# Eight of sixteen on-chip copies of one batch issued from ACT's queue instead of SP's, in a fused attention and expert kernel

## The chip, the cores and the metric

One core of one Trainium2 chip runs the whole program. The metric is the device time of one execution in microseconds (us); less is better. Before the change the median of three runs is 466.92 us (466.87 to 467.25).

The core has five instruction streams that run at once, each in order: TensorE (PE), VectorE (DVE), ScalarE (ACT), GpSimd (POOL) and SyncE (SP). They wait for each other on semaphores. DMA transfers are issued by an instruction on one of these streams and then run by themselves; in the kernel before, SP issues all of them.

## The reference

```python
def sm_attn(qq, kk, vv):
    s = scale * np.matmul(qq, kk.transpose(0, 1, 3, 2))
    s = s - np.max(s, axis=-1, keepdims=True)
    a = np.exp(s)
    a = a / (np.sum(a, axis=-1, keepdims=True) + 1e-09)
    return np.matmul(a, vv)
p_packed = sm_attn(p, k, v)            # 32 packed queries for each head
out = sm_attn(q, p_packed, p_packed)   # 576 queries for each head
...
h = np.maximum(np.maximum(x @ w1, x @ w2), x @ w3)   # x: 4608 x 512, w: 512 x 768
return (h @ w_out).astype(np.float32)
```

There are 8 batches, 8 heads, 576 rows and a head width of 64, all in float32.

## The kernel before, in words

The batches b = 0 to 7 go through the same stages, and the stages of neighbouring batches are interleaved by hand. A stage is a Python generator; one word of a table runs it to its next `yield`, so the table is the order in which every engine gets its instructions. `START` (lines 48 to 73) holds batches 0 and 1 and the beginning of batch 2, and also the words `w` and `C` that load and convert the weights of the two expert layers. `LOOP` (lines 77 to 85) holds one round for each of b = 2 to 7. A word is a letter of a stage, the batch, and further indices.

The stages that matter here:

- `A` (`weigh`, line 261): the exponentials of the packed queries' scores, 128 x 576, in two tiles `a`. For batches 0 and 1 they are transposed on PE (`turn`, line 286).
- `X` (`spread`, line 305): from batch 2 on, DVE transposes 32 x 32 blocks into `x` (line 313), and sixteen SBUF-to-SBUF DMAs move these blocks to the partitions where PE wants them, in the tile `xt` (line 319). Eight of them move 5 blocks and eight 4 blocks for each of 32 partitions. A batch's third word `X` emits the sixteen DMAs.
- `V` (`values`, line 324): 80 small matmuls `av` with `xt` as their weights (line 337), a scaling on DVE to `pp`, then `K` (`packed`, line 349): a transpose on PE (line 352) and a copy to `pt`.
- `Q` (`queries`, line 356): the second scores, with `q` tiles that `load_q` (line 169) brought from memory (issue at line 174).
- `P` and `N` (`project`, `layer_in`): the first expert layer. Its sums `mi` (line 475) are most of PE's work; `E` (`maximum`, line 481) copies the first sum out of PSUM on ACT or DVE (`copy`, lines 129 and 131) and takes the maximum with the others on DVE (line 489).
- `C` (`convert`, line 177): two activations on ACT (lines 188 and 193), a shift on DVE (line 202) and an add on POOL (line 206) put the words of a weight block `wi` in order. `load_w` (issue at line 153) fetches the next `wi` into one of six slots.

The stretch of `START` in which batch 2's DMAs are emitted is this (lines 60 and 61); its `X2` is the third one:

```
... P05 N05 N05 N05 E040
w60 C60 B10g B10 B11 H00 N10 C61 E041 P11 Z20 E050 H00v X2 C60 C60 E041 C61 E050 P11 V201 Z21 V201 N11 N11 K2
```

`N05` are the sums of block 5, `E050` starts with the copy of the first of them on ACT, `V201` runs the `av` matmuls, and `w64`, `w65`, `q21`, `q20`, `w62`, `w63` in the next line are loads issued by SP.

The pool tag `b` has eight slots. The `q` tiles of batch 2 reuse slots that the `av` matmuls and the sixteen DMAs read, so these loads wait for both.

Of the kernel before, what the change touches and what calls it, by code (L numbers as in the profile page):

```python
# [20 lines left out]
B, H, S, D, NP = 8, 8, 576, 64, 32  # L21
# [67 lines left out]
def fused_kernel(ctx: ExitStack, tc: tile.TileContext, kp, qt, va, vb, wi, wo, out):  # L89
# [14 lines left out]
    nc = tc.nc  # L104
# [200 lines left out]
    def spread(b):  # L305

        x = pool.tile([P, NT, R, NP], F32, name=f"x{b}", tag="b", bufs=NB)
        for r in range(R):
            nc.vector.transpose(out=x[:, :, r], in_=a1[b, r][0].rearrange("p (t y) -> p t y", y=NP))
            yield 1
        at = pool.tile([P, SF + 1, 4, R, NP], F32, name=f"xt{b}", tag="b", bufs=NB)
        for c in range(4):
            n = len(range(c, NT, 4))
            for i in range(4):
                nc.sync.dma_start(out=at[NP * c:NP * c + NP, 0:n, i], in_=x[NP * i:NP * i + NP, c::4])  # L319
        for r in range(R):  # L320
            a1t[b, r] = at[:, :, :, r]
        yield 0
# [282 lines left out]
    def weigh_and_turn(b, r):  # L605
# [4 lines left out]

    stages = {
        "S": scores, "A": weigh_and_turn, "Z": invert, "X": spread, "V": lambda b, *rs: values(b, rs), "K": packed, "Q": queries,
        "B": attend, "C": convert, "P": project, "N": layer_in, "E": maximum, "H": halves,
        "O": layer_out, "F": finish, "W": weights,
# [77 lines left out]
```

## Time and profile before

| | |
|---|---|
| time, median of three runs | 466.92 us (466.87 to 467.25) |
| span of the profiled execution | 464.4 us |
| PE busy | 455.2 us (98%) |
| DVE busy | 333.5 us (72%) |
| POOL busy | 247.9 us (53%) |
| ACT busy | 159.9 us (34%) |
| DMA queues | 55.66 MB, all of the kernel's own transfers on one queue |

The time of the profiled execution itself is not listed beside its span. The span runs from the first to the last instruction, and the median of the three runs is 2.5 us longer than it. Busy times are sums over the span. DMA issues are not counted as busy, so ACT's and SP's streams can be occupied where the table shows nothing. An engine that waits shows up as the idle time before an instruction, with the engine or DMA that ended it; the chain of waits follows these back from the last instruction.

### The profile page before, as it was taken

What the parts mean: (1) busy time and instruction counts of PE and PEld (TensorE: products, weight loads), DVE (VectorE), ACT (ScalarE), POOL (GpSimd) and SP (SyncE); (2) the same over time, 40 slices, a digit from 0 to 9 for tenths busy, and PEclk for the clock granted to TensorE, in tenths of its full rate; (3) what the DMA queues carried; (4) which work ended last, traced back from release to release, by engine and by line L of the source; (5) the groups of instructions that cost most, each with busy time, mean ns of one, the idle gap of its engine ahead of it and who ended that gap; (6) DMA issues with size and microseconds to landing.
All of it is one profiled execution on the core that took longest, in us unless ns stands there. A gap on an engine that the chain in (4) does not pass through costs nothing.

```text
span 464.4 us, 11561 instructions
## 1 busy us (share of the span) xinstructions
PE 455.2 (98%) x4724; PEld 404.9 (87%) x4724; DVE 333.5 (72%) x698; ACT 159.9 (34%) x341; POOL 247.9 (53%) x213
## 2 busy tenths in 40 slices
PE   7999998999999999999999999999999999999996
PEld 3477887899899898998899988998989988998996
DVE  1799987888887678566887479766786668845552
ACT  2787856535322126022331025121260223302130
POOL 0468875574542675526572384706764275725832
PEclk9999999999999999999999999999999999999999
DMA  8999846010316430256004450065202540020002
GB/s 313 398 382 355 321 98 230 1 58 25 95 66 195 135 119 1 80 160 233 2 27 152 87 211 2 27 199 155 94 1 94 151 116 1 28 76 1 2 6 97
DMA packets 35780, 55.66 MB, mean 120 GB/s; under 512 B 17296, under 2 KB 26512, under 8 KB 35728
## 3 DMA queue, kind: packets, MB, share of 16 engines
q1 hardware_dynamic: 35728, 54.93, 35.4%
q8 instruction: 37, 0.61, 0.5%
q14 instruction: 15, 0.12, 0.1%
HBM read 41.94 MB, written 9.44 MB: 111 GB/s over the span
## 4 chain that ended last, share of the span: by engine, by line
PE 88%; DMA 5%; SPq 3%; DVE 3%; issue 1%; ACT 1%; DVEq 0%
PE mi L475 44%; PE mo L544 29%; PE pw L439 6%; PE idle L143 2%; SPq L319 2%; PE s L366 2%; PE av L337 2%; DMA wi<-in_wi 2%; PE s L253 2%; DMA q<-in_qt 1%; DMA kt<-in_kp 1%; PE tp L296 0%; DMA xt<-x 0%; SPq L159 0%; PE pa L337 0%
## 5 line engine op out<-in xcount | busy, mean ns | idle before, releaser
L475 PE MATMUL mi<-a2h,ph 128*128 128x288 f32 x576 | 173.5, 301 | 0.8 <-DVE pl L452 0.6
L475 PE MATMUL mi<-a2l,ph 128*128 128x288 f32 x576 | 169.9, 295 | 0.0
L475 PE MATMUL mi<-a2h,pl 128*128 128x288 f32 x576 | 169.6, 295 | 0.0
L489 DVE TENSOR_TENSOR r<-mi,r 128x288 f32<-128x288 f32 x192 | 84.4, 452 | 57.8 <-PE mi L475 55.3
L475 PEld LDWEIGHTS mi<-a2h,ph 128*128 128x128 f32 x576 | 108.0, 188 | 13.4 <-issue 7.0
L475 PEld LDWEIGHTS mi<-a2l,ph 128*128 128x128 f32 x576 | 108.0, 188 | 0.2
L475 PEld LDWEIGHTS mi<-a2h,pl 128*128 128x128 f32 x576 | 108.1, 188 | 0.0
L513 POOL TENSOR_TENSOR r<-r 128x288 f32<-128x288 f32 (+1 forms) x47 | 50.4, 1083 | 81.3 <-DVE r L489 65.5
L129 ACT COPY r<-mi 128x288 f32<-128x288 f32 x73 | 29.0, 399 | 185.8 <-PE mi L475 185.7
L450 ACT ACTIVATE ph<-pw 128x384 fp32r<-128x384 f32 (+1 forms) x67 | 40.2, 631 | 46.5 <-PE pw L439 43.5
L452 DVE SCALAR_TENSOR_TENSOR pl<-pw,ph 128x384 fp32r<-128x384 f32 (+1 forms) x67 | 46.2, 713 | 9.5 <-ACT ph L450 9.2
L544 PE MATMUL mo<-ych,xl 128*128 128x288 f32 x144 | 42.5, 295 | 0.0
L544 PE MATMUL mo<-ych,xh 128*128 128x288 f32 x144 | 42.4, 294 | 0.0
L544 PE MATMUL mo<-ycl,xh 128*128 128x288 f32 x144 | 42.3, 294 | 0.0
L439 PE MATMUL pw<-w_sb,pt 64*32 64x384 f32 x768 | 36.3, 487 | 0.1
L206 POOL TENSOR_TENSOR w_sb<-w_sb,wi 128x512 int32<-128x512 int32 x18 | 23.9, 1336 | 22.0 <-DVE w_sb L202 17.4
L134 POOL TENSOR_TENSOR ybl<-r,ybh 128x576 fp32r<-128x576 f32 x15 | 21.7, 1448 | 19.7 <-DVE ybh L131 16.2
L134 POOL TENSOR_TENSOR ycl<-r,ych 128x864 fp32r<-128x864 f32 x12 | 26.6, 2218 | 5.1 <-PE mi L475 2.4
L544 PE MATMUL mo<-yah,xh 128*128 128x288 f32 x96 | 28.9, 301 | 0.0
L544 PE MATMUL mo<-yal,xh 128*128 128x288 f32 x96 | 28.4, 296 | 0.2 <-DVE yal L134 0.2
L544 PE MATMUL mo<-ybh,xh 128*128 128x288 f32 x96 | 28.3, 295 | 0.0
L544 PE MATMUL mo<-yah,xl 128*128 128x288 f32 x96 | 28.3, 295 | 0.0
(123 smaller groups left out, 808.4 us busy)
## 6 DMA issues: line engine op xcount, KB each, us to landing
kt<-in_kp SPq DMA_DIRECT2D x16, 640.0 KB, 5.4
q<-in_qt SPq DMA_DIRECT2D x16, 576.0 KB, 5.6
wi<-in_wi SPq DMA_DIRECT2D x18, 512.0 KB, 8.6
v<-in_va SPq DMA_DIRECT2D x16, 512.0 KB, 5.7
wi<-in_wo SPq DMA_DIRECT2D x6, 512.0 KB, 6.7
out_t<-r SPq DMA_DIRECT2D x8, 288.0 KB, 2.2
out_t<-t SPq DMA_DIRECT2D x8, 288.0 KB, 2.3
out_t<-s SPq DMA_DIRECT2D x8, 288.0 KB, 2.7
```

Of the source, the lines that this page charges most:

```text
L129: e.copy(out=out, in_=src)
L134: on(default).tensor_tensor(out=lo, in0=src, in1=hi.bitcast(F32), op=ALU.subtract)
L143: nc.tensor.matmul(out=ps[:, 0:n * P], lhsT=ident, rhs=ident.unsqueeze(1).to_broadcast([P, n, P]), start=True, stop=True,)
L206: nc.gpsimd.tensor_tensor(out=dst.bitcast(I32), in0=dst.bitcast(I32), in1=up, op=ALU.add)
L253: nc.tensor.matmul(out=s1[b][r][32 * n:32 * n + 32, hf, 0:HS], lhsT=kt[g][o, w:w + NP], rhs=kt[g][o, pr * S + hf * HS:pr * S + (hf + 1) * HS],
L439: nc.tensor.matmul(out=ps[r][NP * n:NP * n + NP, 0:NW * P], lhsT=pt_sb[b % 2][o, NP * n:NP * n + NP], rhs=w_sb[o, j, n * NW * P:(n + 1) * ...
L450: nc.scalar.activation(out=hi[:, r], in_=x, func=AF.Copy, scale=2.0 ** -WS)
L452: nc.vector.scalar_tensor_tensor(out=lo[:, r], in0=x, scalar=2.0 ** -WS, in1=hi[:, r].bitcast(F32), op0=ALU.mult, op1=ALU.subtract,)
L475: nc.tensor.matmul(out=sums[b, j, hf, x][:, 0:HS], lhsT=w[:, r, x * P:(x + 1) * P], rhs=a[:, c], start=(r == 0 and n == 0), stop=(r == R - ...
L489: nc.vector.tensor_tensor(out=h, in0=sums[b, j, hf, i][:, 0:HS], in1=h, op=ALU.max)
L513: less = lambda out, x, y: on("g").tensor_tensor(out=out, in0=x, in1=y, op=ALU.subtract)
L544: nc.tensor.matmul(out=ps[:, 0:HS], lhsT=w[:, x, m * P:(m + 1) * P], rhs=h[:, z], start=(p == 0 and i == 0), stop=(p == NQ - 1 and i == 2),)
```

## The change

```diff
@@ -316,7 +316,9 @@
         for c in range(4):
             n = len(range(c, NT, 4))
             for i in range(4):
-                nc.sync.dma_start(out=at[NP * c:NP * c + NP, 0:n, i], in_=x[NP * i:NP * i + NP, c::4])
+                (nc.sync if b > 2 or i < 2 else nc.scalar).dma_start(
+                    out=at[NP * c:NP * c + NP, 0:n, i], in_=x[NP * i:NP * i + NP, c::4],
+                )
```

For batch 2 alone, the DMAs with i = 2 and i = 3 are issued on ACT's stream; those with i = 0 and i = 1 stay on SP's. Batches 0 and 1 have no such DMAs, and batches 3 to 7 keep all sixteen on SP. Line numbers after line 319 grow by two.

On SP, around batch 2's DMAs (`xt` is written from `x`; the `wi` rows before are `w61` and `w60`, those behind are `w64` and `w65`), the piece of the difference is:

```order
 L153 DMA wi_1_959<-in_wo 128x512
 L153 DMA wi_0_990<-in_wo 128x512
-L319 DMA xt_1019<-x_820 32x5x64 x8
-L319 DMA xt_1019<-x_820 32x4x64 x8
+L319 DMA xt_1019<-x_820 32x5x64 x4
+L319 DMA xt_1019<-x_820 32x4x64 x4
 L153 DMA wi_4_1105<-in_wo 128x512
 L153 DMA wi_5_1121<-in_wo 128x512
```

The two weight loads stand eight DMAs nearer to the front of SP's stream.

On ACT, at the same place of the program, the kernel before has this (the bracket lists the engines and DMA counters that an instruction waits for; `mi0_5_0_0` is the first sum of `N05`):

```order
L450 ACTIVATE ph1_1_1010<-pw1_1_857 128x768 [waits PE_49,Activation_49]
L129 COPY r0_2_928<-mi0_5_0_0_968 128x288 [waits PE_49]
L193 ACTIVATE wi6_0_990<-wi6_0_990 128x512
L188 ACTIVATE wi6_5_1121<-wi6_5_1121 128x512 [waits DMAHW3_49,Pool_49]
L193 ACTIVATE wi6_5_1121<-wi6_5_1121 128x512
L129 COPY pt0_73<-av2_1043 128x128 [waits PE_49]
```

and the change has this:

```order
L452 ACTIVATE ph1_1_1010<-pw1_1_857 128x768 [waits PE_49,Activation_49]
L129 COPY r0_2_928<-mi0_5_0_0_968 128x288 [waits PE_49]
L319 DMA xt2_1019<-x2_820 32x5x64 [waits DMAHW7_49,DMAHW4_49]
L319 DMA xt2_1019<-x2_820 32x5x64 [waits DMAHW5_49]
L319 DMA xt2_1019<-x2_820 32x5x64 [waits DMAHW6_49]
L319 DMA xt2_1019<-x2_820 32x5x64 [waits DMAHW7_49]
L319 DMA xt2_1019<-x2_820 32x4x64 [waits DMAHW0_49]
L319 DMA xt2_1019<-x2_820 32x4x64 [waits DMAHW1_49]
L319 DMA xt2_1019<-x2_820 32x4x64 [waits DMAHW2_49]
L319 DMA xt2_1019<-x2_820 32x4x64 [waits DMAHW3_49]
L193 ACTIVATE wi6_0_990<-wi6_0_990 128x512
L188 ACTIVATE wi6_5_1121<-wi6_5_1121 128x512 [waits Pool_49]
```

The eight DMAs stand behind the copy of `mi0_5_0_0` and ahead of the conversions of `w60` and `w65`. The counters DMAHW2 and DMAHW3 are those of the loads `w64` and `w65` at that point, so the last two of ACT's DMAs wait for these loads to land. The orders of PE, DVE and POOL do not change.

## Rows read from the trace of the kernel before

**Rows 1.** The page: span, PE's busy time, the granted clock in 40 slices.
```profile
span 464.4 us, 11561 instructions
...
PE 455.2 (98%) x4724; PEld 404.9 (87%) x4724; DVE 333.5 (72%) x698; ACT 159.9 (34%) x341; POOL 247.9 (53%) x213
...
PEclk9999999999999999999999999999999999999999
```

**Rows 2.** Who waited for whom, PE: us in total, times, longest us.
```profile
PE s L366 <- DMA q<-in_qt: 1.3, 1, 1.3
```

**Rows 3.** The chain of waits around batch 2's transfers: start us, us, what.
```profile
54.84 0.73 SPq L319
...
61.24 0.60 SPq L319
61.84 0.04 issue
61.88 0.60 SPq L319
...
65.49 1.93 DMA xt<-x
67.42 0.04 issue
67.47 1.51 PE av L337 x74
...
69.49 6.43 DMA q<-in_qt
```

**Rows 4.** Line 319 between 40 and 80 us: issue ns min/median/max, who waited, landing.
```profile
L319 SPq DMA_DIRECT2D xt<-x x16: 585/602/1017, 54.8 to 65.5; - x16
...
  PEld av L337: 0.3, 1
```

**Rows 5.** Timeline of SP: start us, us, line, operation [idle before].
```profile
54.84 11.26 SPq L319 DMA_DIRECT2D xt<-x  x16
66.20 1.01 SPq L153 DMA_DIRECT2D wi<-in_wo  x2
68.93 0.88 SPq L174 DMA_DIRECT2D q<-in_qt  x2
```

**Rows 6.** Timeline of ACT from 65 us, same columns.
```profile
65.08 0.40 ACT L129 COPY r<-mi 128x288 f32<-128x288 f32 x1
65.35 0.70 ACT L193 ACTIVATE wi<-wi 128x512 int32<-128x512 uint32 x1
73.17 0.68 ACT L188 ACTIVATE wi<-wi 128x512 f32<-128x512 f32 x1 [7.12 <-DMA wi<-in_wo]
```

**Rows 7.** Timeline of PE between 60 and 78 us, same columns.
```profile
60.47 0.88 PE L439 MATMUL pw<-w_sb,pt 64*32 64x384 f32 x16
...
64.44 0.30 PE L475 MATMUL mi<-a2l,ph 128*128 128x288 f32 x1
...
74.48 0.29 PE L475 MATMUL mi<-a2l,ph 128*128 128x288 f32 x1
76.06 1.21 PE L366 MATMUL s<-q,pt 64*32 64x288 f32 x32 [1.28 <-DMA q<-in_qt]
```

**Rows 8.** Line 174, all loads of q: issue ns min/median/max, landing us.
```profile
L174 SPq DMA_DIRECT2D q<-in_qt x16: 327/328/536, 1.6 to 375.5; - x16
...
DMA to landing us min/median/max: 4.1/5.6/9.2
```

**Rows 9.** Timeline of POOL: the additions that free the slots of w64, w65.
```profile
50.64 4.14 POOL L206 TENSOR_TENSOR w_sb<-w_sb,wi 128x512 int32<-128x512 int32 x3 [0.75 <-ACT wi L188]
```

**Rows 10.** Line 153 between 60 and 90 us: landing of the weight loads.
```profile
DMA to landing us min/median/max: 4.2/6.7/7.3
```

**Rows 11.** Timeline of PE, its first work in the span.
```profile
1.36 3.83 PE L143 MATMUL s<-ident 128*128 128x512 f32 x6 [1.36 <-POOL ident masks.py:199]
...
8.26 2.21 PE L143 MATMUL idle<-ident 128*128 128x512 f32 x6
```

## The prediction

> **What bounds the kernel now.** I read the page first. PE is busy 455.2 of 464.4 us, at the full granted clock in every slice [rows 1], so a change outside PE counts only where PE waits, or where it comes to wait. The list of waits comes next. Besides its start, the longest wait of PE's matmuls is 1.3 us before the second scores of batch 2, ended by the load of `q` [rows 2]. PE's weight loads also wait 0.3 us for `xt` in this stretch [rows 4]. The chain of waits shows how these two belong together [rows 3]: sixteen issues on SP from 54.84 us, the last of them from 65.49 us and landed 1.93 us later, `av` on PE from 67.47 us, then the load of `q` for 6.43 us. SP's timeline has nothing but these issues for 11.26 us, and behind them the two weight loads at 66.20 us [rows 5]. So sixteen issues are a real queue, but PE pays only 0.3 us for it, because it has other sums to do until about 67.1 us.
>
> **The change, part by part.**
>
> *Eight issues leave SP.* SP's issues follow each other by 0.64 us [rows 3]. With eight of them the run of 11.26 us becomes half, and SP is free at about 54.84 + 5.6 = 60.4 us. What PE needs from these eight lands by about 62 us, 5 us before PE gets to it, so by itself this gains at most PE's 0.3 us, and only if the other eight are as early.
>
> *The other eight go to ACT, and there they come late.* The order puts them behind ACT's copy of the first sum of `N05`. That copy ran from 65.08 us and ended at 65.48 us [rows 6]. It could not be earlier than its sum: after the projection at 60.47 us, PE does four groups of six sums, the fourth is this one, and the 24th matmul ends at 64.44 + 0.30 = 64.74 us [rows 7]. ACT's stream is in order, so the first of its DMAs is issued between 64.74 us (the copy is waited for but not finished) and 65.48 us (finished). I take 65.1 us, where the copy starts, since the activations in these rows start before the one ahead has ended. In the kernel before, SP was issuing its last DMA at that time.
>
> *What an issue on ACT takes* is not in the trace, as ACT issues no DMA there. The nearest rows are SP's issues of the same transfers, 585 to 1017 ns with a median of 602 [rows 4] and 0.64 us from one to the next; I take that, as nothing in the transfer changes. The cheapest DMA issue of the rows is that of `q`, 327 ns [rows 8]. I keep 0.33 us and 1.02 us as ends.
>
> *The sum for `av`.* Start of the eighth issue: 65.1 + 7 x 0.64 = 69.6 us. Landing, 1.93 us later: 71.5 us. PE starts the third and fourth of the `av` matmuls, which read i = 2 and i = 3, 0.05 us behind: 71.55 us in place of 67.47 us, or **+4.1 us**. PE has nothing it could do instead: the first four `av` matmuls want all four i, and its order does not change. The earliest and latest start with issues of 0.585 and 0.70 us (the mean of SP's run, 11.26 / 16) give +3.3 and +4.9 us; ends of 0.33 and 1.02 us give +1.9 and +6.7 us.
>
> *ACT's own work.* Eight issues hold ACT for some 5.1 us, until 70.2 us. In the kernel before it stood idle for 7.12 us there, until the load of `w65` landed at 73.17 us [rows 6]; only the conversion of `w60`, at 65.35 us, stands behind the DMAs and moves to about 70.2 us. POOL needs it for an addition, and the result is read later than 75 us. I cost it at nothing: that idle time covers it, and PE has moved by 4.1 us as well. Were the cover gone, the price would be the 5 us by which ACT is held.
>
> *The weight loads `w64` and `w65`* move from 66.20 to about 60.5 us. Their slots were freed by the three additions that end at 50.64 + 4.14 = 54.78 us [rows 9], so nothing holds them. ACT's last two DMAs wait for them to land. With the longest landing in this stretch, 7.3 us [rows 10], the later one is there by about 61.1 + 7.3 = 68.4 us, ahead of ACT's seventh issue at 68.9 us. Cost nothing, with little to spare.
>
> *The load of `q` and the wait that is paid back.* `q` waits for the `av` matmuls to release its slot, so its issues move with PE from 68.93 to 73.05 us, the second one from 69.49 to 73.6 us. Before, it took 6.43 us because `w64` and `w65`, issued 2.7 us earlier, were still on the way. Now they have long landed. The median of all `q` loads is 5.6 us, the shortest 4.1 us [rows 8]; with 5.5 us `q` is there at 79.1 us. PE ends its sums at 74.77 us before [rows 7], 78.9 us now. The wait of 1.28 us shrinks to about 0.2 us: **-1.0 us**, between 0 and -1.28 us. `pt`, the other thing that the second scores want, was copied by ACT behind the late conversion of `w65`; now it is earlier against PE, not later.
>
> *Behind that* PE is busy without long waits to the end, and all of its work moves by what is left. Sum: +4.1 - 1.0 = **+3.1 us**, on a span of 464.4 us; the median of the three runs is 2.5 us above that span, and I carry the same amount over: 466.92 + 3.1 = **470.0 us**. Its own bounds are +3.3 - 1.28 and +4.9 - 0, so 469.0 to 471.8 us.
>
> **The rivals.**
>
> *Faster: ACT's issues do not stand behind its activations.* If ACT's stream can send a DMA on while the activations listed before it still wait for PE, the eight go out beside SP's from 54.84 us on, and all sixteen have landed by about 62 us. PE's 0.3 us at `av` goes, and `q` finds the weight loads out of its way: 5.5 us in place of 6.43 us, so some 1.1 us of its wait go. That gives 466.92 - 1.4 = 465.5 us. The point that decides is when ACT's last DMA is issued: before about 66.5 us the loss at `av` is below what `q` gives back. For it speaks that the DMAs in the listing wait only for DMA counters; against it, that ACT is an in-order stream and the copy before them waits for PE until 64.74 us. The Trainium skill (Perfetto Trace Analysis, DMA Optimizations) says that where an issuing engine looks busy with slices, spreading DMAs over the engines that can issue may help. SP's row of 11.26 us is such a picture, and by that rule this rival would hold; what the rule leaves out here is where the second queue stands in its own program when the data is ready. Chance 0.06.
>
> *No change: an issue on ACT is cheap.* At 0.33 us each, PE restarts at 65.1 + 7 x 0.33 + 1.93 + 0.05 = 69.4 us, +1.9 us, and 1.0 us is given back: 467.8 us. No row speaks for it but that of `q`, which has another shape. Chance 0.10, over half of it within 0.2%.
>
> *Slower still: PE's clock falls in the stall.* PE would stand for some 4.4 us, from 67.1 to 71.55 us; no wait in the trace is nearly as long, and the granted clock is full throughout [rows 1]. But PE's first work after the start of the span was slow: 10 blocks of 128 columns in 3.83 us, where 9 blocks later take 2.21 us [rows 11]. That is 1.4 us more than 10 / 9 x 2.21. If the stall ends in the same way, PE loses about 1.4 us, and the remaining wait for `q` is swallowed: 470.0 + 1.4 - 0.2 = 471.2 us. The Trainium skill (TensorE: Matmul & The Clock Gate, Part 1) says that an idle PE falls back to 1.2 GHz and needs sustained work to get 2.4 GHz again. No row before shows that within the span. Chance 0.20.
>
> **How the numbers follow.** The forecast has 0.64, the rivals 0.06, 0.10 and 0.20. A difference of 0.2%, or 0.93 us, is about what a measurement of this kernel can tell from none. Slower by more than that: the forecast, the clock and a little less than half of the cheap issue, 0.88; within it 0.06; faster 0.06. The range runs from 468.3 us, between the cheap issue and the forecast's lower bound, to 472.6 us, which takes in the clock's case and an issue of 1.02 us (466.92 + 6.7 - 1.0). It leaves out the faster rival, most of the cheap issue and the sum of all upper bounds.
>
> **What would show it.** In the changed profile ACT's eight issues should start between 64.7 and 65.5 us, 0.64 us apart; PE's weight loads for `av` should wait for a DMA of `xt` for some 4.4 us; the 1.3 us before the second scores should have shrunk; and `w64` and `w65` should be issued near 60 us. I am wrong if ACT's first issue comes before 61 us, if the issues lie closer than 0.3 us, or if PE's wait for `xt` stays below 1 us. A granted clock below full behind the stall would be the third rival.

## The result and the profile after

The change makes the kernel slower: **471.69 us** (median of four runs, 470.80 to 472.20) against 467.01 us (466.87 to 467.25) before. The ratio is 1.0109, with an interval from 1.0097 to 1.012. The prediction was 470.0 us in a range from 468.3 to 472.6, with slower as the likeliest outcome. So the sign and the range held, and the time is 1.7 us above the forecast, close to the 471.2 us of the rival with the falling clock.

The profiled execution of the change took 471.64 us with a span of 469.8 us. The span before was 464.4 us, 5.4 us shorter, while the medians differ by 4.7 us. All executions listed with both figures took 1.8 us more than their span, so the execution profiled before must have been one of some 466.2 us, below its median. Part of the 2.5 us that the prediction carried from span to median was this, not an overhead.

The page of the change answers to [rows 1]. PE's busy time rose by 3.9 us with the same 4724 matmuls, and one slice of the granted clock shows a 7 (a digit is tenths, and 9 means 90% or more):

```profile
span 469.8 us, 11563 instructions
PE 459.1 (98%) x4724; PEld 407.3 (87%) x4724; DVE 334.0 (71%) x698; ACT 160.3 (34%) x341; POOL 247.9 (53%) x213
PEclk9999997999999999999999999999999999999999
```

SP's timeline (start us, us, line, operation), to be held against [rows 5]:

```profile
54.82 6.07 SPq L319 DMA_DIRECT2D xt<-x  x8
61.00 1.00 SPq L153 DMA_DIRECT2D wi<-in_wo  x2
```

SP is free at 60.9 us, and `w64` and `w65` go out at 61.0 instead of 66.2 us. ACT's timeline, same columns, against [rows 6]:

```profile
64.93 0.71 ACTq L319 DMA_DIRECT2D xt<-x  x1
65.18 0.40 ACT L129 COPY r<-mi 128x288 f32<-128x288 f32 x1
65.68 4.52 ACTq L319 DMA_DIRECT2D xt<-x  x7
70.25 0.66 ACT L193 ACTIVATE wi<-wi 128x512 int32<-128x512 uint32 x1 [4.68 <-DMA xt<-x]
```

The eight issues start at 64.93 us and follow each other by about 0.65 us. The chain of waits gives the end of that row, start us, us, what:

```profile
69.59 1.93 DMA xt<-x
```

The eighth transfer is issued at 69.59 us, lands 1.93 us later, and PE goes on at 71.61 us. PE's timeline, against [rows 7] (the bracket is the idle time before, and what ended it):

```profile
67.13 0.31 PE L339 MATMUL av<-v,xt 128*32 128x64 f32 x4
70.97 0.39 PE L339 MATMUL av<-v,xt 128*32 128x64 f32 x2 [3.53 <-DMA xt<-x]
71.61 2.47 PE L339 MATMUL av<-v,xt 128*32 128x64 f32 x74 [0.26 <-DMA xt<-x]
74.42 0.44 PE L477 MATMUL mi<-a2h,pl 128*128 128x288 f32 x1
77.00 0.27 PE L354 MATMUL av<-ident,pp 128*128 128x128 f32 x1
77.24 0.29 PE L477 MATMUL mi<-a2h,pl 128*128 128x288 f32 x1
81.17 1.20 PE L368 MATMUL s<-q,pt 64*32 64x288 f32 x32
```

PE stands for 3.8 us in two pieces. What follows is slow: the last 74 `av` matmuls take 2.47 us where they took 1.51 [rows 3], and a sum's matmul 0.44 us where it takes 0.29 a little later. From the restart to the transpose `av<-ident` PE needs 77.00 - 71.61 = 5.39 us. The wait before the second scores `s`, 1.28 us in [rows 7], is gone.

The table of stretches says why. Its columns are the stretch, its length, then busy time and number of instructions for PE, PE's weight loads, DVE, ACT and POOL, then the granted clock, the DMA share and GB/s:

```profile
68.00:70.00 2.00, 0.00 (x0) 0.00 (x0) 0.20 (x2) 0.00 (x0) 1.92 (x3) 1.00 0.31 57
70.00:72.00 2.00, 0.78 (x18) 0.60 (x22) 0.00 (x0) 1.75 (x3) 1.84 (x2) 0.52 0.18 33
72.00:74.00 2.00, 2.00 (x70) 1.67 (x61) 0.00 (x0) 0.04 (x1) 0.29 (x1) 0.50 0.03 8
74.00:76.00 2.00, 2.00 (x12) 1.99 (x9) 0.62 (x3) 0.00 (x0) 0.00 (x0) 0.50 0.42 90
76.00:78.00 2.00, 2.00 (x14) 2.00 (x13) 1.11 (x4) 0.27 (x1) 0.00 (x0) 0.77 0.99 380
78.00:80.00 2.00, 2.00 (x17) 2.00 (x16) 1.83 (x6) 0.98 (x2) 0.00 (x0) 1.00 0.96 351
```

While PE stood, from 70 us on, its granted clock fell to 0.50, the lower of its two levels (1.2 and 2.4 GHz), and it came back to 1.00 at about 77 us. The digits of [rows 1] say only 90% or more for the kernel before; the view of its cores gives the mean of its profiled execution:

```profile
core 0: 464.4 us, clock 1.000
```

There the transpose came sooner after `av`. That row of PE's timeline before was not among those shown:

```profile
70.53 0.27 PE L352 MATMUL av<-ident,pp 128*128 128x128 f32 x1
```

PE starts its row of 74 records with the fourth `av` matmul, the first that reads i = 3 (the profile lists each of the 40 matmuls as two records). So from there, at 67.47 us [rows 3], it took 70.53 - 67.47 = 3.06 us, and the change needs 5.39 us for the same work. The sum of what PE lost is 71.61 - 67.47 = 4.14 us for the late transfers, plus 5.39 - 3.06 = 2.33 us for the clock, less the 1.28 us of `q`'s wait: 5.19 us. The second scores start at 81.17 us instead of 76.06, which is 5.11 us.

The load of `q`, from the view of its tile (issue ns, first and last start; then from issue to landing):

```profile
L174 SPq DMA_DIRECT2D q<-in_qt x2: 322/325/328, 74.1 to 74.7; - x2
DMA to landing us min/median/max: 3.8/4.2/4.7
```

Before, the second of these loads took 6.43 us [rows 3]. Whether the earlier weight loads are the reason is one of the questions below.

### The profile page after: what moved, and what is told of

Its sections match the earlier page's. It is cut to its first block, busy times and chain, and to the rows that moved or that the text cites. A ratio compares the mean times of both kernels' runs of the same rounds, so it can differ in the third digit from the quotient of the medians.

```text
span 469.8 us, 11563 instructions
## 1 busy us (share of the span) xinstructions
PE 459.1 (98%) x4724; PEld 407.3 (87%) x4724; DVE 334.0 (71%) x698; ACT 160.3 (34%) x341; POOL 247.9 (53%) x213
## 4 chain that ended last, share of the span: by engine, by line
PE 90%; DMA 4%; DVE 2%; ACT 2%; ACTq 1%; issue 1%; POOL 0%; SPq 0%
PE mi L477 48%; PE mo L546 28%; PE pw L441 7%; DMA wi<-in_wi 4%; PE av L339 2%; PE s L253 2%; PE s L368 2%; ACTq L319 1%; ACT wi L188 1%; DMA xt<-x 0%; DVE r L491 0%; ACT ph L452 0%; DVE pl L454 0%; POOL w_sb L206 0%; PE tp L339 0%
```

## The experiments

The theory after the result: the restart of `av` is set by ACT's late issues, as predicted; the clock that fell in PE's stall costs 2.3 us more; `q`'s wait went because `w64` and `w65` left earlier. The rivals: the slow matmuls have another cause than the stall; `q`'s wait was swallowed by PE's slow stretch; the number of issues, and not their place in ACT's stream, is what counts. Each kernel was timed beside the kernel before on the same chip (medians of 465.99, 466.42 and 466.78 us), and ratios are to these.

This table holds the readings from PE's timeline in all of them: PE's wait at `av` for `xt` (the sum of its parts; the profile names no releaser for the one in the last line), when the 74 to 80 `av` matmuls behind it began, the time from there to the transpose, and PE's wait for `q`, in us. "Late" is the place of the change in ACT's stream, "early" one described further down.

| kernel | time | ratio (interval) | wait `xt` | `av` from | to transpose | wait `q` |
|---|---|---|---|---|---|---|
| before | 467.01 | | 0.3 (weight loads) | 67.47 | 3.06 | 1.28 |
| the change: 8 late | 471.69 | 1.0109 (1.0097 to 1.012) | 3.8 | 71.61 | 5.39 | 0 |
| 8 late, PE kept busy | 470.63 | 1.0099 (1.0077 to 1.0121) | 0.37 | 71.13 | 3.03 | 0.85 |
| 6 late | 469.44 | 1.0063 (1.004 to 1.0086) | 2.6 | 70.44 | 4.51 | 0 |
| 4 late | 468.60 | 1.0052 (1.0034 to 1.007) | 2.3 | 69.89 | 4.05 | 0 |
| 2 late | 470.97 | 1.0089 (1.006 to 1.0119) | 3.4 | 70.72 | 5.45 | 0 |
| 2 late, weights behind | 466.40 | 0.9986 (0.9971 to 1.0001) | 0.33 | 67.44 | 3.03 | 1.18 |
| 8 late, weights behind | 471.93 | 1.0112 (1.0093 to 1.013) | 3.7 | 71.55 | 5.47 | 0 |
| 8 late, PE busy, weights behind | 470.74 | 1.0092 (1.0064 to 1.012) | 0.33 | 71.61 | 3.06 | 0.61 |
| 8 early | 470.90 | 1.0087 (1.0069 to 1.0106) | 0 | 72.84 | 3.07 | 0 |
| 3 early | 465.90 | 0.9987 (0.9976 to 0.9997) | 0 | 67.13 | 3.07 | 0.91 |
| 4 early | 465.79 | 0.9975 (0.9961 to 0.999) | 0 | 66.92 | 3.07 | 0.51 |
| 4 early, weights first | 466.78 | 0.9998 (0.9978 to 1.0017) | 0.39 | 68.39 | 3.07 | 1.10 |

### Is it the stall that slows PE?

The change, with sixteen blocks of unused matmuls put on PE ahead of the `av` products, in the table of the order:

```diff
-... E050 P11 V201 Z21 V201 N11 N11 K2
+... E050 P11 I16 V201 Z21 V201 N11 N11 K2
```

> The change, with sixteen blocks of 128 columns of idle matmuls put on PE just ahead of batch 2's av matmuls (about 3.9 us of work that nothing uses, in the place of PE's stall). Theory (late transfers plus a fallen clock): the transfers of xt land as late as in the change, av goes on near 71.6 us, but the granted clock stays at 1.00, av and the twelve sums behind it take 1.5 and 1.6 us again in place of 2.5 and 3.1; 471.7 - 2.4 = 469.3 us. Rival (the slow stretch behind the stall comes from something else, such as ACT's late conversions or transfers in SBUF): PE stays slow there and the time stays at 471.7 us.

PE's timeline there, columns as above:

```profile
66.54 3.61 PE L143 MATMUL av<-ident 128*128 128x384 f32 x12
...
71.13 1.41 PE L339 MATMUL av<-v,xt 128*32 128x64 f32 x74 [0.37 <-DMA xt<-x]
79.26 1.20 PE L368 MATMUL s<-q,pt 64*32 64x288 f32 x32 [0.85 <-DMA q<-in_qt]
```

Stretches of this kernel, columns as in the table of stretches above:

```profile
70.00:72.00 2.00, 1.53 (x66) 1.18 (x64) 0.00 (x0) 1.58 (x3) 1.65 (x2) 1.00 0.10 17
72.00:74.00 2.00, 2.00 (x39) 1.82 (x29) 0.91 (x3) 0.00 (x0) 0.00 (x0) 1.00 0.39 57
```

The transfers came no earlier (`av` went on 16.82 us after SP's first issue, and 16.79 us in the change), but the granted clock was 1.00 where the change had 0.52 and 0.50, the 74 records took 1.41 us and the way to the transpose 3.03 us, as before. So PE's standing still is what made it slow. The end shows less of it: 470.63 us, with an interval that overlaps that of the change. From SP's first issue (54.31 us here, 54.82 in the change) to the second scores it is 24.95 against 26.35 us, so 1.40 of the 2.33 us were saved there, and the wait for `q` took back 0.85. From there to the end of the span it is 468.4 - 79.26 = 389.14 us against 388.63, so half a microsecond more was lost later. The other kernel with the unused matmuls shows 389.08 us and the kernels without them 388.3 to 388.6. Why is not shown.

### How many issues, and what else moves

The change with six, four and two transfers of batch 2 on ACT, at the same place:

```diff
-(nc.sync if b > 2 or i < 2 else nc.scalar).dma_start(
+(nc.sync if b > 2 or i < 2 or (i == 2 and c < 2) else nc.scalar).dma_start(
```

```diff
-(nc.sync if b > 2 or i < 2 else nc.scalar).dma_start(
+(nc.sync if b > 2 or i < 3 else nc.scalar).dma_start(
```

```diff
-(nc.sync if b > 2 or i < 2 else nc.scalar).dma_start(
+(nc.sync if b > 2 or i < 3 or c < 2 else nc.scalar).dma_start(
```

> Six of the sixteen on ACT. Late transfers: ACT's sixth issue starts near 68.3 us and lands near 70.2 us, PE restarts at 70.3 us, 2.8 us later than before; the wait for q (1.3 us) is paid back. With the clock held: 467.0 + 1.5 = 468.5 us; with the clock fallen as in the change: about 470.7 us. Rival (a cost in proportion to the issues on ACT): 467.0 + 4.7 x 6 / 8 = 470.5 us, with no stall at av to show for it.

> Four on ACT (those with i = 3). Late transfers: the fourth issue near 67.0 us, landed 68.9 us, PE restarts 1.5 us later than before, the wait for q is paid back, the clock holds: 467.0 + 0.2 = 467.2 us. Rival (in proportion): 469.4 us.

> Two on ACT (i = 3 of the last two c). Late transfers: the second issue near 65.7 us, landed 67.6 us, PE restarts 0.2 us later than before; the weight loads w64 and w65 go out 1.8 us earlier than before and some 1.0 us of the wait for q is paid back: 467.0 - 0.8 = 466.2 us. Rival (in proportion): 468.2 us.

With six, the products went on 1.2 us earlier than with eight, two issues less. With four it should have been as much again, but only 0.55 us came. The chain of waits has the last of the four slower to land (start us, us, what):

```profile
67.11 2.69 DMA xt<-x
```

And with two, where nothing was to be lost, PE waited 3.39 us and the time was back near that of the change. Here is the chain of waits with two (start us, us, what):

```profile
65.58 5.01 DMA xt<-x
...
70.72 2.47 PE av L339 x74
```

The second transfer was issued at 65.58 us and took 5.01 us to land, where others take 1.9 to 2.0. SP's timeline has the weight loads out just before it:

```profile
54.71 9.72 SPq L319 DMA_DIRECT2D xt<-x  x14
64.54 1.00 SPq L153 DMA_DIRECT2D wi<-in_wo  x2
```

In the stretch from 68 to 69 us the DMA engines are full (the last two columns, DMA share and GB/s):

```profile
68.00:69.00 1.00, 0.00 (x0) 0.00 (x0) 0.13 (x1) 0.00 (x0) 1.00 (x2) 1.00 1.07 422
```

The theory formed on this: two weight loads of 512 KB, which a freed SP sends out early, fill the DMA engines just when ACT's small transfers start. With four they had left at 64.06 us, just ahead of ACT's first transfer at 65.08, which fits the 2.69 us of ACT's last. In the change they had left at 61.0 us and were out of the way; in the kernel before they left behind the last transfer. The test takes them out of SP's stream and issues them on ACT behind the two transfers:

```diff
+(nc.scalar if j == NJ and c > 3 else nc.sync).dma_start(out=t, in_=wi[j, c] if j < NJ else wo[c])
```

> Two of the sixteen transfers on ACT as in the experiment with two, which took 470.97 us, but w64 and w65 are issued on ACT's queue behind these two, and no longer by SP at 64.5. Theory (the two weight loads of 512 KB each, which a free SP issues early, slow ACT's small transfers): without them ACT's second transfer, issued near 65.6, lands some 2 us later, near 67.6; PE waits 0.3 to 0.7 us for it where it waited 3.39, its granted clock holds at 1.0, the products of av take 1.5 us, and q's wait of PE is back with 1 to 2 us. That makes 467 us (466.3 to 468). Rival (ACT's queue itself is slow for these transfers, whatever else the DMA carries): the second transfer lands again about 5 us after its issue, PE restarts near 70.7 and the time stays at 470 to 471.

The chain of waits of this kernel, and below it a row of ACT's timeline:

```profile
65.36 1.94 DMA xt<-x
...
67.44 1.41 PE av L339 x74
```

```profile
66.11 1.12 ACTq L153 DMA_DIRECT2D wi<-in_wo  x2
```

The same transfer, issued on the same queue at the same place, lands in 1.94 us; PE waits 0.33 us, its clock holds, `q`'s wait is back with 1.18 us, and the time is that of the kernel before. So it was the weight loads and not ACT's queue, and some 4.8 us by the ratios (1.0089 and 0.9986) hung on whether these loads were issued just before the two transfers or just behind them. The Trainium skill (DMA: Bandwidth & Descriptors, Issuing engines are not separate DMA queues) says that DMAs run on the same 16 engines and interleave, whichever engine starts them; the 5.01 against 1.94 us agree. It adds that issuing on several engines saves only the time of issuing, usually small against the transfer itself. Here it is not small: eight issues of 0.65 us stand against a landing of 1.93 us.

With four transfers the clock fell in an unexpected way. Rows of the stretches there, columns as above:

```profile
71.00:71.50 0.50, 0.50 (x18) 0.41 (x15) 0.10 (x1) 0.00 (x0) 0.50 (x2) 1.00 0.00 0
71.50:72.00 0.50, 0.50 (x4) 0.50 (x4) 0.37 (x2) 0.00 (x0) 0.50 (x1) 0.67 0.00 0
72.00:73.00 1.00, 1.00 (x6) 1.00 (x6) 0.26 (x1) 0.00 (x0) 0.26 (x1) 0.50 0.78 129
```

PE was back at work at 69.89 us after 2.3 us of waiting, did its 74 records of `av` in 1.41 us, and only then, near 71.7 us, the clock went to 0.50. With six it fell near 71.6 us, 1.2 us after the restart. So the cost of a stall can come after it, in work that has nothing to do with it.

### What became of `q`'s wait

The prediction had it shrink because `w64` and `w65` left SP earlier. In the next kernel all eight transfers are on ACT as in the change, but the two loads are issued on ACT behind them (at 70.30 us), so that they leave later than before.

> The change, with the two weight loads w64 and w65 issued by ACT behind its eight transfers, so that they are again some 3 us ahead of the loads of q, as in the kernel before. Theory (the wait for q was paid back because these loads had left): they go out near 70.3 to 71.3 us, q takes 6 us or more again in place of 4.7, pt is copied behind the late conversion of w65, and 1 to 1.5 us of wait before the second scores come back: 471.7 + 1.2 = 472.9 us. Rival (the wait went because PE itself was slow after the stall): no wait, 471.7 us.

The wait did not come back, though the second `q` load now took 6.2 us (the view of its tile):

```profile
DMA to landing us min/median/max: 4.0/5.1/6.2
```

PE was in its slow stretch, and came to the second scores at 81.46 us, later than `q`. To see the loads' effect with the clock held, the unused matmuls were added:

> The change with the sixteen idle blocks of matmuls on PE ahead of the products (they change no value), and with w64 and w65 issued on ACT behind the eight transfers. This gives the price of the weights' earlier departure with the clock held. Theory: q's wait is 1.3 to 1.8 us where it was 0.85 with SP's early issue, and the time 0.4 to 1.0 us above the 470.63 of the experiment with idle matmuls alone. Rival (the earlier departure is worth the whole 1.0 of the prediction, or nothing): the wait is 1.9 us or more, or 0.9 or less.

```profile
79.52 1.20 PE L368 MATMUL s<-q,pt 64*32 64x288 f32 x32 [0.61 <-DMA q<-in_qt]
```

The wait was 0.61 us, not longer than the 0.85 us with the loads issued early, and the time the same within its interval. That is one end of the rival, worth nothing: with the clock held, the earlier departure bought nothing that can be seen. What sets the landing of `q` stays open. It took 4.7 to 4.9 us at most in the change and in the kernels with six, four and two late transfers and eight early ones, and 5.2 to 6.4 us in all others.

### The place in ACT's stream

If the place is what hurts, the same issues on ACT should cost less where ACT can send them before PE's sum of `N05` is due. For that, a `yield` splits the stage: ACT's transfers are emitted by an additional word on the line before, and SP's by the old one.

```diff
-... E021 w61 C61 E031 P05 E041 P05 N05 N05 N05 E040
+... E021 w61 C61 E031 X2 P05 E041 P05 N05 N05 N05 E040
...
+        on_act = [(1, 3), (2, 3), (3, 3)] if b == 2 else ()
+        if b == 2:
+            for c, i in on_act:
+                move(nc.scalar, c, i)
+            yield 0
+        for c in range(4):
+            for i in range(4):
+                if (c, i) not in on_act:
+                    move(nc.sync, c, i)
```

With the eight of the change (`on_act` holds all c with i = 2 and 3):

> The change's eight on ACT, emitted at the same earlier place. Theory: issues from about 60.5 to 65.6 us, landed near 67.5 us, so the stall at av nearly goes; but ACT's next activation, which makes the operand of block 5's sums, moves from 61.5 to 65.6 us, and PE waits for it and for DVE's step behind it: a stall of about 3.3 us some 3 us earlier, and 1.3 to 1.6 us paid back: 467.0 + 1.7 = 468.7 us, or about 471 us if the clock falls. Rival (ACT's hold costs nothing, only lateness does): 465.6 us.

ACT's timeline, then PE's:

```profile
60.43 5.74 ACTq L320 DMA_DIRECT2D xt<-x  x6
66.22 0.81 ACT L460 ACTIVATE ph<-pw 128x768 fp32r<-128x768 f32 x1 [5.68 <-DMA xt<-x]
```

```profile
67.37 0.40 PE L485 MATMUL mi<-a2h,ph 128*128 128x288 f32 x1 [3.67 <-ACT r L129]
```

All transfers are there in time, but now ACT's own work stands behind them. The activation `ph`, from 61.5 us in the other kernels, starts at 66.22, and PE waits 3.67 us for a copy on ACT. The granted clock fell there too (0.66 from 68 to 70 us, 0.50 to 72). The chain of waits shows that issuing is only a part of this hold:

```profile
61.10 4.45 DMA xt<-x
...
65.58 0.59 ACTq L320
```

ACT's last issue waited until 65.56 us for an earlier transfer to land. That transfer took 4.45 us, and SP had sent out `w64` and `w65` at 60.86 us, just ahead of it. So the weight loads have a part in this stall as well; how the time would come out without them was not tried. Eight on ACT cost about the same at either place, by two different ways: once PE waits for the last transfer, once for what ACT does behind it.

With three:

> Three on ACT (i = 3 of c = 1, 2, 3), emitted earlier in ACT's program: behind the first conversion step of w61, where ACT waits for PE from 60.8 to 61.5 us in the kernel before. Theory (only the place in ACT's program decides): ACT's issues run from about 60.5 to 62.4 us and land before 64.5 us, SP's thirteen end near 64 us and land by 65.5 us, so PE does not wait for xt at all (0.3 us gained); w64 and w65 go out 2 us earlier, and the 1.3 us before the second scores go: 467.0 - 1.6 = 465.4 us, faster than both kernels. Rival (issues on ACT cost by themselves): at or above 467 us. ACT's next activation is delayed by some 0.8 us; if PE waits for it, up to 0.5 us of the gain is lost.

ACT's timeline:

```profile
59.16 0.72 ACTq L320 DMA_DIRECT2D xt<-x  x1
...
59.92 0.61 ACTq L320 DMA_DIRECT2D xt<-x  x1
60.16 0.68 ACT L188 ACTIVATE wi<-wi 128x512 f32<-128x512 f32 x1
61.55 0.81 ACT L460 ACTIVATE ph<-pw 128x768 fp32r<-128x768 f32 x1 [0.71 <-PE pw L449]
```

Here ACT has time for them: `ph` starts at 61.55 us and waits for PE as before. No wait for `xt` is left, `w64` leaves at 65.56 us, and `q`'s wait is 0.91 us. With 0.9987 this is just faster than before. With four:

> As the experiment with three transfers on ACT at the early place (465.9 us), with a fourth, all four of i=3. Theory: SP ends its twelve issues 0.6 us earlier and w64 leaves 0.6 us earlier, so q's wait falls from 0.91 to 0.3 to 0.6, and 465.5 us come out; ACT's own work there starts up to 0.6 us later, which lies beside PE's work. Rival (SP waits for a counter that a transfer shares with the load of w60, so that nothing leaves earlier): the same 465.9 or up to 0.5 more.

SP's timeline, then PE's:

```profile
54.61 10.52 SPq L320 DMA_DIRECT2D xt<-x  x12
```

```profile
66.92 1.46 PE L347 MATMUL av<-v,xt 128*32 128x64 f32 x80
74.75 1.21 PE L376 MATMUL s<-q,pt 64*32 64x288 f32 x32 [0.51 <-DMA q<-in_qt]
```

At 465.79 us and a ratio of 0.9975 (0.9961 to 0.999) it beats both kernels, by little: five of the 29 executions of the kernel before that it is compared with had a mean granted clock of 0.995 or 0.996 and took 468.2 to 469.1 us, and without these five the medians are 465.79 and 466.46 us. That four are better than three is not shown, as their intervals overlap. From SP's first issue to the second scores it is 20.14 us, 1.08 less than before (76.06 - 54.84 = 21.22): 0.3 from `av`, 0.77 from `q`. SP was not freed as much as expected, though: its twelve issues still took 10.52 us, since one waited 2.1 us for a transfer of `xt` to land, through a DMA counter.

Last, the weight loads ahead of SP's twelve (the words `w64` and `w65` right behind `w60`):

> The four transfers of i=3 go on ACT at the early place of the experiment with three, and SP issues w64 and w65 right behind w60, ahead of its own twelve transfers. Theory (q's wait is set by when w64 is issued): w64 lands several us before PE asks for q, the wait of 1.3 us (0.91 with three on ACT) is gone, SP's twelve transfers end near 65.5 to 66.5 and are landed before PE needs them at 67.1 if the loads have drained by then; 465.0 us, some 1.5 below the kernel before. Rival (the loads slow the small transfers, as with two on ACT): the last transfers land after 67.1 by 1 to 4 us, PE waits for them that long, and 467 to 470 us come out.

SP's waits name the cost:

```profile
SPq L320 <- DMA wi<-in_wo: 3.0, 1, 3.0
```

SP's issues now wait for the counters of the loads. The first transfer behind the loads takes 6.6 us to land, which is early enough; the last one goes out at 66.4 us and lands 1.9 us later, and the bulk of `av` starts at 68.39 us. `q` is waited for with 1.10 us although `w64` and `w65` have long landed. The gain is gone at 466.78 us. That is the rival's stall, 1.2 us late, but by another way than it said: the last transfers are not slow, they are issued late. And it is a second sign that these weight loads do not set `q`'s wait.

## Why the prediction was right or wrong

*Eight issues leave SP, and the weight loads move up:* right. SP was free at 60.9 us (60.4 forecast) and the loads went out at 61.0 (60.5).

*ACT's issues come late:* right. First at 64.93 us (between 64.74 and 65.48, 65.1 taken), 0.65 us apart with 613 ns as the median of one (0.64 and 602 ns taken from SP), landing 1.93 us, PE back at 71.61 us (71.55). The term was +4.1 us and measured +4.14. The faster rival needed ACT to send its transfers before about 66.5 us, and fell. But it had a grain of truth: with three early, a transfer listed behind the conversion that ran at 60.16 us started at 59.16, one microsecond ahead of it. ACT's stream can issue a DMA before the activations listed ahead of it have run, though at the late place it did not before the wait of one ahead was over (PE's sum ended at 64.83 us, the first issue started at 64.93). The cheap issue fell too, at 0.65 us.

*ACT's own work costs nothing:* right at this place. The conversion of `w60` moved to 70.25 us, POOL waited 0.16 us for it, and PE not at all. The price named for the case without cover, 5 us of ACT's hold, is what eight on ACT at the early place showed as PE's 3.67 us, there with the weight loads' part in it.

*PE's clock:* this is the step that failed. The forecast let PE run at full speed behind the stall; the rival with the clock had 0.20. The mechanism was as described there, the size was not: 1.4 us came from a row of PE's first work, and 2.33 us were measured. That row compared only ten slow blocks, and the view of stretches shows 1.00 for it, so the trace does not show it as a row at the lower clock; in the change the granted clock stayed at 0.50 from about 70 to 77 us, over both the `av` products and the sums behind them. By the forecast's own rows (no wait of PE nearly as long) a fall could not be excluded. In the profiled executions every kernel that made PE wait for 2.3 us or more lost clock, while waits of up to 1.28 us lost none. The order of the program alone does not decide it: with six late, one of four executions had a mean clock of 0.999 and took 467.93 us, the others 0.995 or 0.996 and 469.26 to 470.00 us, and five executions of the kernel before had lost some too, as said above. Why those five did is not known. The Trainium skill (TensorE: Matmul & The Clock Gate, Part 1) says that an idle PE falls back to 1.2 GHz, and the trace agrees with its 0.50.

*`q`'s wait is paid back with 1.0 us:* the amount was near, the reason was not. In the change all 1.28 us went, and the kernel with the weights behind shows that the slow stretch alone is enough for that. With the clock held, the wait was 0.85 us with the weights early and 0.61 us with them late, so 0.4 to 0.7 us are gained, and not by their earlier departure.

*The sum.* +4.14 + 2.33 - 1.28 = +5.2 us on the rows, where +4.1 - 1.0 = +3.1 was forecast. The medians moved by 4.7 us. The stated range held because its upper end was drawn to take in the clock. That 471.69 us also lies inside the forecast's own bounds, 469.0 to 471.8 us, is luck: they were drawn for later or dearer issues and for a wait of `q` that stays, and none of these came.

## What to carry to other kernels

A second queue saves nothing by itself: look up where its issues stand in the issuing engine's own program, what that engine waits for ahead of them and who waits for what stands behind them, and move only as many as fit in a gap there, three or four of sixteen in this case and at an earlier place. Ask as well what the freed queue sends next, because a large load that moves up can hold small transfers back for longer than the queue did. Price a wait of the matrix engine with the clock behind it: here waits of 2.3 us and more cost 1 to 2.4 us on top, those of up to 1.28 us nothing. Where between the two it begins is not shown.

## What was not expected of the hardware

Two loads of 512 KB, the first of them issued about 1 us before it, made a small on-chip transfer take 5.01 instead of 1.94 us, with the DMA share at 0.94 to 1.07 from 67 to 69 us. After stalls of 2.3 to 2.6 us PE first ran at full speed again, and its clock fell to 0.50 one to two microseconds later. And ACT's stream issued a DMA a microsecond ahead of an activation listed before it (59.16 against 60.16 us).
